# Linear attention into a SoLU layer on one core: w_out means on VectorE, tiles in any PSUM bank, and a new order

## The chip, the cores and the metric

The kernel runs on one core of a Trainium2 chip. The core has a matrix engine (TensorE, PE in the profile, with its weight loads as PEld), VectorE (DVE), ScalarE (ACT), GpSimd (POOL) and SyncE (SP), which work side by side, each through its own queue in program order, and wait for each other by semaphores. Matrix products land in PSUM, which has eight banks. The metric is the device time of one execution in microseconds (us), lower is better.

## The reference

Eight batches of eight heads with 576 tokens of 64 numbers; then one layer on the 4608 tokens of 512 numbers.

```python
kv = np.einsum('bhsd,bhse->bhde', k, v)
out = np.einsum('bhsd,bhde->bhse', q, kv)
rms = np.sqrt(np.mean(out * out, axis=-1, keepdims=True) + 1e-06)
x = (out / rms * g_norm)            # heads side by side: 4608 x 512
h = x @ w_in                        # 512 x 1024
e = np.exp(h - h_max)
solu = h * (e / (np.sum(e, axis=-1, keepdims=True) + 1e-09))
ln = (solu - mu) / np.sqrt(var + 1e-06) * g_ln
return ln @ w_out                   # 1024 x 512
```

## The kernel before, in words

The 4608 tokens are worked in nine chunks of 512, called c. Chunk c below 8 holds the first eight of every nine tokens of batch c; chunk 8 holds the ninth ones of all batches. A step's name carries its chunk: u.2.5 is the product u of chunk 2, piece 5.

For each batch, k, v and q are loaded by POOL's DMA queue with a cast to bf16 (`load`, L292; for batches 0 and 1 in two halves of four heads each). `kv_mm` (L333) multiplies k by v on 64 x 64 tiles; `kv_copy` (L346) brings the result to SBUF in two layouts, kvd[..., 0] and kvd[..., 1], in which the two heads of a pair lie in either half of the partitions. For batches 0 and 1 the matmuls give one layout only, and of three copies per half one is whole and two carry the crossed halves over. q is turned by PE (`qT_mm`, L368) for chunks 0 to 3 and by a transposing DMA on SP for the others. `o_mm` (L385) gives the attention output o, half hf and part z at a time. ACT squares it (sq), `s_mm` averages it over the head, ACT makes the reciprocal root (ln and ex; one instruction in chunk 0), and DVE multiplies (x, L422). So x of a chunk has four pieces, hf 0 and 1 by z 0 and 1.

The layer: `h_mm` (L459) multiplies the four row blocks of w_in by x for each of eight pieces f of 128 features; for chunks 0 to 2 each piece is cut in a first half (row blocks 0 and 1, which need only hf 0) and a second (2 and 3). ACT takes exp (L466), DVE multiplies h by it to u (L470), u is squared on POOL or ACT (usq, L474), and POOL adds pairs of exps (es, L478). `sums` (L498) adds u, usq and es over the features with 80 small matmuls; `turn`, `stats` and `rstd` make one scale per token from them. The softmax's divisor and the layer norm become that scale together with a mean taken out of w_out beforehand: w_out is loaded as fp32r (w_out_f), `w_mean` (L540) computes the mean over the features of g_ln times w_out with eight matmuls against g_mean, and `w_center` (L546) writes g_ln times w_out less that mean in bf16. `out_mm` (L557) multiplies u by it, four blocks m of 128 tokens a chunk; `scale` (ob, L564) multiplies by the token's scale, and `store` (L568) sends the block out, from SP's queue or, at the end, ACT's.

The last block, out.8.3, is computed in one bank; its scaling and store are cut in two halves of 256 columns (L590).

What sets the order of the work: every step is a named piece, and the string ORDER (L20) is one list by hand of all pieces; `emit` (L133) issues them in that order, so each engine's queue is the list cut down to its own pieces, POOL's and SP's DMA issues among them. A word such as usq.0.4:act picks the engine. PSUM is held by tags: h, out and o have two banks each, s and misc one each; HOME (L89) moves single tiles to another tag. A tile may take a bank when the earlier user of it is done. "warm" (L272) are matmuls on zeros with no use for the result: twelve at the start, then seven times two between the first steps. make_ident (L259) builds the identity on POOL behind seven loads; turn_g (L263) and all of PE behind it wait for that.

## Time and profile before

| | |
|---|---|
| median of 3 runs | 193.65 us (193.42 to 195.79) |
| span of the profiled execution, first to last instruction | 192.3 us |
| busy: PE, ACT, POOL, DVE | 93%, 76%, 67%, 58% |
| mean granted TensorE clock | 0.982 |
| moved by DMA | 29.71 MB, mean 154 GB/s |

Of the profiled execution the page gives the span; the runs' times also hold what lies before the first and after the last instruction. In the lines that follow, a group's line has line number, engine, operation, tiles written and read, shapes and count, then busy us and mean ns of one, then the idle time of the engine just before these instructions and who ended it. A matmul's mean holds its way through the array; a row of them follows each other faster: 12 of 128x512 take 2.59 us at full clock. A line of the windows has the stage, its length, busy us and count of PE, PEld, DVE, ACT and POOL, the granted clock, the share of the DMA engines and GB/s. A line of the timeline has start, duration, engine, line, operation and in brackets the idle time before it and its releaser.

### The profile page before, as it was taken

The numbers are of one execution on the slowest core, as the hardware profiler recorded it, in microseconds if no ns is written. First come the engines' busy times: TensorE is split into PE (matmuls) and PEld (weight loads), VectorE is DVE, ScalarE is ACT, GpSimd is POOL, SyncE is SP. The second block draws the span as 40 slices with busy tenths as digits, with TensorE's granted clock in tenths as the row PEclk, the third lists the DMA queues.
The fourth block names the chain that finished last, engine by engine and source line by source line (L and its number), as shares of the span: only waits on it lengthen the run. The fifth ranks groups of instructions, "written<-read, shape, count | busy, mean of one in ns | idle before, by whom it ended". The sixth has DMA issues, their size and how long they took to land.

```text
span 192.3 us, 5320 instructions
## 1 busy us (share of the span) xinstructions
PE 179.1 (93%) x2199; PEld 88.1 (46%) x2199; DVE 110.8 (58%) x228; ACT 146.3 (76%) x256; POOL 129.6 (67%) x138
## 2 busy tenths in 40 slices
PE   7697996999799999998999999999999999999991
...
PEclk9879998899999999999999999999999999999999
...
GB/s 51 187 205 206 206 336 290 208 207 209 206 185 186 241 162 200 201 271 176 170 209 251 33 16 197 201 81 111 75 15 55 29 139 0 109 112 0 162 61 218
DMA packets 35544, 29.71 MB, mean 154 GB/s; under 512 B 16440, under 2 KB 30016, under 8 KB 35520
## 3 DMA queue, kind: packets, MB, share of 16 engines
...
q10 hardware_dynamic: 144, 0.13, 0.2%
...
## 4 chain that ended last, share of the span: by engine, by line
PE 70%; DMA 9%; POOL 6%; ACT 5%; DVE 4%; issue 4%; POOLq 0%; ACTq 0%
PE h_ps L461 26%; PE out_ps L559 25%; DMA k_sb<-in_k_dram 9%; PE misc_ps L505 5%; PE o_ps L392 3%; PE s_ps L404 3%; ACT osq_sb L211 2%; PE misc_ps L340 2%; PE misc_ps L373 2%; POOL v_sb L295 2%; DVE x_sb L424 2%; PE out_ps L542 1%; PE s_ps L275 1%; POOL k_sb L295 1%; ACT e_sb L468 1%
## 5 line engine op out<-in xcount | busy, mean ns | idle before, releaser
L461 PE MATMUL h_ps<-x_sb,w_in_sb 128*128 128x512 bf16 x288 | 70.4, 381 | 0.1
L559 PE MATMUL out_ps<-w_out_sb,u_sb 128*128 128x512 bf16 x288 | 68.9, 379 | 0.1
L213 POOL TENSOR_TENSOR usq_sb<-u_sb 128x512 bf16<-128x512 bf16 x52 | 53.4, 1040 | 21.3 <-DVE u_sb L472 21.2
L472 DVE TENSOR_TENSOR u_sb<-h_ps,e_sb 128x512 bf16<-128x512 f32 x72 | 47.5, 685 | 23.0 <-ACT e_sb L468 19.9
L480 POOL TENSOR_TENSOR es_sb<-e_sb 128x512 bf16<-128x512 f32 x36 | 45.4, 1275 | 20.2 <-issue 11.9
L468 ACT ACTIVATE e_sb<-h_ps,zero_t 128x512 f32<-128x512 f32 x72 | 46.6, 687 | 11.7 <-PE h_ps L461 9.1
L559 PEld LDWEIGHTS <-u_sb 128*128 128x128 bf16 x288 | 27.4, 98 | 33.7 <-issue 2.1
L461 PEld LDWEIGHTS <-w_in_sb 128*128 128x128 bf16 x288 | 26.9, 98 | 32.2 <-issue 2.8
L424 DVE SCALAR_TENSOR_TENSOR x_sb<-o_ps,g_rep,rst_sb 128x512 bf16<-128x512 f32 x36 | 26.6, 747 | 19.8 <-ACT rst_sb L412 17.2
L211 ACT ACTIVATE osq_sb<-o_ps,zero_t 128x512 bf16<-128x512 f32 x36 | 23.3, 685 | 5.6 <-PE o_ps L392 5.6
L408 ACT ACTIVATE lss_sb<-s_ps,eps_t 128x512 f32<-128x512 f32 x32 | 21.2, 685 | 3.3 <-PE s_ps L404 3.1
L219 DVE TENSOR_SCALAR ob_sb<-out_ps,rstd 128x512 f32<-128x512 f32 (+1 forms) x21 | 15.3, 734 | 14.0 <-PE out_ps L559 11.0
L412 ACT ACTIVATE rst_sb<-lss_sb,zero_t 128x512 f32<-128x512 f32 x32 | 22.5, 720 | 0.4
L404 PE MATMUL s_ps<-osq_sb,head_mean 128*128 128x512 bf16 x36 | 13.5, 392 | 1.9 <-ACT osq_sb L211 1.9
L211 ACT ACTIVATE usq_sb<-u_sb,zero_t 128x512 bf16<-128x512 bf16 x20 | 13.8, 715 | 1.0 <-DVE u_sb L472 1.0
L505 PEld LDWEIGHTS <-stat_sel 128*32 128x32 bf16 x720 | 10.3, 97 | 5.4 <-issue 5.3
L217 ACT ACTIVATE ob_sb<-out_ps,rstd 128x512 f32<-128x512 f32 (+1 forms) x16 | 10.5, 672 | 2.5 <-PE out_ps L559 2.0
L207 ACT CAST kvd<-misc_ps 64x128 bf16<-64x128 f32 (+1 forms) x13 | 3.4, 260 | 10.9 <-PE misc_ps L340 8.2
L207 DVE CAST kvd<-misc_ps 64x128 bf16<-64x128 f32 (+1 forms) x17 | 4.9, 288 | 11.3 <-ACT kvd L207 11.0
L275 PE MATMUL s_ps<-zeros 128*128 128x512 bf16 x26 | 9.3, 495 | 1.2 <-DVE zeros L238 1.2
L392 PE MATMUL o_ps<-qT_sb,kvd 64*64 64x256 bf16 (+1 forms) x192 | 8.6, 253 | 1.7 <-DVE kvd L207 1.3
L340 PEld LDWEIGHTS <-k_sb 64*64 64x64 bf16 x576 | 7.1, 110 | 4.7 <-issue 3.8
...
## 6 DMA issues: line engine op xcount, KB each, us to landing
...
k_sb<-in_k_dram POOLq DMA_DIRECT2D x4, 288.0 KB, 10.5
...
```

Of the source, the lines that this page charges most:

```text
L211: nc.scalar.activation(out=dst, in_=src, func=AF.Square, bias=zero_t[:, :])
L213: on[engine].tensor_tensor(out=dst, in0=src, in1=src, op=MUL)
L404: nc.tensor.matmul(t[:, :], head_mean[:, :], T["osq", i][:, :], start=True, stop=True)
L408: nc.scalar.activation(out=t[:, :], in_=T["s", i][:, :], func=AF.Ln, bias=eps_t[:, :])
L412: nc.scalar.activation(out=t.rearrange("p a b c -> p (a b c)"), in_=T["lss", i][:, :], func=AF.Exp, scale=-0.5, bias=zero_t[:, :])
L424: nc.vector.scalar_tensor_tensor(out=t[:, 2 * hf:2 * hf + 2, z], in0=T["o", c, hf, z][:, :, :, :], scalar=g_rep[:, :], in1=T["rst", (c, hf ...
L461: nc.tensor.matmul(bank(("h", c, f), [128, 512])[:, :], w_in_sb[:, dt, f * 128:(f + 1) * 128], T["x", c][:, dt].rearrange("p a b c -> p (a ...
L468: nc.scalar.activation(out=t[:, f % 2, :], in_=T["h", c, f][:, :], func=AF.Exp, bias=zero_t[:, :])
L472: nc.vector.tensor_tensor(out=t[:, f, :], in0=T["h", c, f][:, :], in1=T["e", c, f // 2][:, f % 2, :], op=MUL)
L480: on[engine].tensor_tensor(out=t[:, n, :], in0=e[:, 0, :], in1=e[:, 1, :], op=ADD)
L505: nc.tensor.matmul(t[32 * j:32 * j + 32, 0, :], stat_sel[:, i, :], cols, start=(part == 0 and n == 0), stop=(part == 2 and n == n_src - 1) ...
L559: nc.tensor.matmul(bank(("out", c, m), [128, d_model])[:, :], T["u", c][:, f, m * 128:(m + 1) * 128], w_out_sb[:, f, :], start=(f == 0), s ...
```

## The change

- w_out is loaded as plain fp32. DVE adds up g_ln times w_out over four blocks at a time (w_add, eight instructions into w_acc and w_accr), and w_mean is one matmul for each half against a constant (mean_r). g_mean goes.
- The tags go: each of the eight banks is a tag of its own, and HOME names a bank for every PSUM tile.
- w_in is loaded in halves of its rows (row blocks 0 and 1, then 2 and 3) instead of its columns.
- For batches 0 and 1 kv_mm computes both layouts into two banks, twice the matmuls, and two whole copies replace the three.
- out.8.3 is computed as two halves of 256 columns in two banks, each with its own ob and store.
- usq may run on DVE. In the new order 35 of the 72 are on POOL, 12 on ACT and 25 on DVE; before it was 52 on POOL and 20 on ACT.
- The fill matmuls are given by FILL (name of the tile whose bank they use, count, columns). 26 of 512 columns stand first in PE's queue.
- ORDER is new throughout. The DMA queue of POOL begins v.0.0, (identity), q.0.0, k.0.0, q.0.1, v.0.1, k.0.1, w_in.0, w_in.1, q.1.0, k.1.0, v.1.0, w_out.1, v.1.1, q.1.1, k.1.1, w_out.0; before, all of batch 1 came ahead of w_out. store.8.1, store.8.2 and store.8.3.1 go by ACT's queue.
- pair_add and its names stand in the code, but PAIRED is empty and no such piece is made.

The diff, cut to its core; of ORDER the first and last lines of either side are shown.

```diff
 ORDER = """
-v.0.0 k.0.0 q.0.0 q.0.1 warm k.0.1 v.0.1 w_in.1 ident turn_g warm.0 kv_mm.0.0 warm.2 qT_mm.0.0 kv.0.0.0:act kv.0.0.1
-kv.0.0.2:act warm.3 qT.0.0 w_in.0 g_mean o_mm.0.0 warm.1 sq.0.0.1 q.1.0 warm.4 v.1.0 sq.0.0.0 s_mm.0.0.1 ex.0.0.1
-qT_mm.0.1 k.1.0 qT.0.1 warm.5 s_mm.0.0.0 kv_mm.0.1 ex.0.0.0 kv.0.1.1:act x.0.0.1 x.0.0.0 kv.0.1.0 kv.0.1.2 q.1.1 k.1.1
-warm.6 o_mm.0.1 sq.0.1.1 sq.0.1.0 v.1.1 s_mm.0.1.1 h.0.6.0 s_mm.0.1.0 h.0.4.0 ex.0.1.1 ex.0.1.0 x.0.1.1 x.0.1.0
-h.0.5.0 w_out.0 h.0.0.0 h.0.5.1 h.0.4.1 table w_out.1 exp.0.5 exp.0.4 h.0.6.1 h.0.1.0 es.0.2 h.0.0.1 exp.0.6 exp.0.0
-h.0.1.1 qT_mm.1.0 h.0.3.0 kv_mm.1.0 h.0.3.1 u.0.5 u.0.6 u.0.4 qT.1.0 u.0.0 exp.0.1 kv.1.0.0:act kv.1.0.2:act kv.1.0.1
-h.0.2.0 o_mm.1.0 qT_mm.1.1 h.0.2.1 h.0.7.0 u.0.1 exp.0.3 qT.1.1 u.0.3 sq.1.0.1 sq.1.0.0 exp.0.2 u.0.2 s_mm.1.0.0
-usq.0.6 h.0.7.1 ln.1.0.0 s_mm.1.0.1 kv_mm.1.1 exp.0.7 q.2.0 ln.1.0.1 kv.1.1.2:act kv.1.1.0 kv.1.1.1 ex.1.0.0 o_mm.1.1
-sq.1.1.1 usq.0.0 usq.0.2 k.2.0 es.0.0 x.1.0.0 ex.1.0.1 s_mm.1.1.1 sq.1.1.0 x.1.0.1 es.0.1 v.2.0 u.0.7 w_mean.0
-ln.1.1.1 s_mm.1.1.0 ex.1.1.1 h.1.5.0 w_mean.1 ln.1.1.0 x.1.1.1 h.1.0.0 w_center.5 ex.1.1.0 x.1.1.0 usq.0.1 h.1.2.0
-v.3.0 usq.0.4:act w_center.2 h.1.6.0 usq.0.7:act w_center.0 qT_mm.2.1 h.1.0.1 v.4.0 h.1.5.1 es.0.3 usq.0.3:act h.1.6.1
-h.1.1.0 h.1.2.1 exp.1.0 usq.0.5 k.3.0 k.4.0 exp.1.5 h.1.1.1 w_center.1 u.1.0 exp.1.6 exp.1.2 qT.2.1:act exp.1.1 u.1.5
...
-u.8.7 u.8.1 store.6.3 store.6.0 store.6.2 out.7.2.0 turn.7 store.6.1 exp.8.3 exp.8.2 out.7.1.0 h.8.5.1 out.7.1.1
-out.7.3.0 exp.8.5 stats.7 rstd.7 out.7.2.1 u.8.2 u.8.5 u.8.3 usq.8.5:act usq.8.2 out.7.3.1 usq.8.7:act out.7.0.0
-es.8.3 ob.7.1 ob.7.2 es.8.1 es.8.2 out.8.0.0 usq.8.1:act ob.7.3:act usq.8.3:act store.7.1 out.8.2.0 usq.8.4:act sums.8
-out.7.0.1 ob.7.0 turn.8 out.8.1.0 store.7.2 out.8.2.1 store.7.3 store.7.0 stats.8 out.8.0.1 out.8.3.0 out.8.1.1 rstd.8
-out.8.3.1 ob.8.2:act ob.8.0 ob.8.1:act store.8.0 store.8.2 store.8.1 ob.8.3.1:act ob.8.3.0 store.8.3.0:act store.8.3.1
+warm.2 warm.9 warm.4 warm.3 v.0.0 warm.0 ident turn_g q.0.0 qT_mm.0.0 qT.0.0 k.0.0 kv_mm.0.0 kv.0.0.1:act q.0.1
+qT_mm.0.1 v.0.1 kv.0.0.0:act qT.0.1 o_mm.0.0 sq.0.0.0 warm.1 g_ln s_mm.0.0.0 warm.6 sq.0.0.1 s_mm.0.0.1 ex.0.0.0
+x.0.0.0 ex.0.0.1 k.0.1 kv_mm.0.1 kv.0.1.0 w_in.0 w_in.1 kv.0.1.1:act o_mm.0.1 sq.0.1.1 warm.5 sq.0.1.0 s_mm.0.1.1
+ex.0.1.1 x.0.0.1 h.0.7.0 s_mm.0.1.0 h.0.0.0 q.1.0 h.0.5.0 ex.0.1.0 x.0.1.1 table h.0.2.0 h.0.3.0 x.0.1.0 h.0.2.1
+exp.0.2 u.0.2 h.0.0.1 exp.0.0 u.0.0 h.0.7.1 exp.0.7 h.0.1.0 h.0.1.1 u.0.7 h.0.5.1 h.0.3.1 exp.0.5 exp.0.1 exp.0.3
+qT_mm.1.0 k.1.0 v.1.0 kv_mm.1.0 kv.1.0.0:act h.0.6.0 w_out.1 qT.1.0 kv.1.0.1 v.1.1 u.0.3 q.1.1 h.0.4.0 u.0.5 o_mm.1.0
+h.0.4.1 k.1.1 u.0.1 w_add.4 sq.1.0.1 sq.1.0.0 h.0.6.1 s_mm.1.0.1 w_out.0 w_add.5 w_add.6 exp.0.6 u.0.6 es.0.3
+s_mm.1.0.0 ln.1.0.0 ex.1.0.0 x.1.0.0 warm.7 exp.0.4 u.0.4 usq.0.0 ln.1.0.1 ex.1.0.1 warm.8 qT_mm.1.1 kv_mm.1.1
+kv.1.1.1:act q.2.0 kv.1.1.0:act qT.1.1 o_mm.1.1 sq.1.1.1 sq.1.1.0 x.1.0.1 h.1.7.0 s_mm.1.1.1 ln.1.1.1 usq.0.1
+s_mm.1.1.0 es.0.0 w_add.7 ln.1.1.0 h.1.6.0 w_add.0 w_add.1 w_add.2 h.1.2.0 v.2.0 h.1.3.0 qT_mm.2.0 ex.1.1.1 k.2.0
+w_add.3 w_mean.0 w_mean.1 x.1.1.1 h.1.5.0 ex.1.1.0 es.0.1 q.3.0 x.1.1.0 qT.2.0:act h.1.3.1 exp.1.3 h.1.1.0 h.1.1.1
+exp.1.1 w_center.0 w_center.1 qT_mm.2.1 usq.0.7:dve usq.0.2 w_center.2 es.0.2 u.1.3 w_center.3 u.1.1 qT.2.1:act
+h.1.7.1 exp.1.7 h.1.5.1 usq.0.4 u.1.7 v.3.0 h.1.2.1 exp.1.2 exp.1.5 h.1.0.0 u.1.5 h.1.6.1 h.1.0.1 exp.1.0 u.1.0
+kv_mm.2.0 exp.1.6 kv.2.0.1:act u.1.2 kv.2.1.1:act h.1.4.0 h.1.4.1 exp.1.4 w_center.4 w_center.5 kv.2.0.2:act usq.0.6
+kv.2.1.0:act usq.0.5 w_center.7 usq.0.3 kv.2.1.2:act out.0.2.0 out.0.2.1 sums.0 kv.2.0.0:act o_mm.2.0 sq.2.0.0 k.3.0
+turn.0 sq.2.0.1 out.0.3.0 out.0.3.1 u.1.6 w_center.6 usq.1.6:dve v.4.0 out.0.3.2 k.4.0 u.1.4 s_mm.2.0.0 ln.2.0.0
+ex.2.0.0 out.0.2.2 out.0.2.3 s_mm.2.0.1 stats.0 rstd.0 out.0.3.3 out.0.0.0 x.2.0.0 usq.1.3 ln.2.0.1 ex.2.0.1 out.0.0.1
+out.0.0.2 ob.0.2 o_mm.2.1 kv_mm.3.0 out.0.0.3 sq.2.1.0 s_mm.2.1.0 usq.1.1:dve es.1.0 usq.1.7:dve x.2.0.1 usq.1.4
...
+turn.7 out.7.0.0 exp.8.2 u.8.2 exp.8.3 u.8.3 stats.7 usq.8.2:dve es.8.1 usq.8.3 out.7.1.0 out.7.1.1 store.6.3 rstd.7
+ob.7.1 store.7.1 h.8.7.1 exp.8.7 out.7.0.1 out.7.3.0 out.7.3.1 ob.7.3:act es.8.0 usq.8.5 out.8.1.0 ob.6.0:act ob.7.0
+out.7.2.0 out.7.2.1 usq.8.0:act ob.7.2:act store.7.0 store.6.0 u.8.4 store.7.3 es.8.3 store.7.2 u.8.7 usq.8.7:dve
+out.8.2.0 usq.8.4:dve usq.8.1:dve sums.8 turn.8 stats.8 rstd.8 out.8.1.1 ob.8.1:act store.8.1:act out.8.0.0 out.8.0.1
+ob.8.0:act store.8.0 out.8.2.1 ob.8.2 store.8.2:act out.8.3.0 ob.8.3.0:act store.8.3.0 out.8.3.1 ob.8.3.1:act
+store.8.3.1:act
 """
...
 HOME = """
-misc.g:s s.warm:misc misc.kv.0.0:h misc.kv.0.1:s misc.kv.1.1:s misc.kv.4.0:s s.kv.4.1:misc misc.kv.5.0:h misc.kv.6.0:h
...
+misc.g:4 misc.kv.0.0.0:6 misc.kv.0.0.1:7 misc.kv.0.1.0:4 misc.kv.0.1.1:5 misc.kv.1.0.0:0 misc.kv.1.0.1:2
...
+out.8.3.1:6 s.warm:4
 """
+FILL = {0: ("s.warm", 19, 512), 1: ("misc.kv.0.0.1", 18, 128), 2: ("o.0.0.1", 2, 512), 3: ("s.0.0.1", 1, 512), 4: ("s.0.0.0", 1, 512), 5: ("misc.kv.0.1.1", 9, 128), 6: ("o.0.1.1", 2, 512), 7: ("misc.kv.1.1.1", 24, 128), 8: ("o.1.1.1", 3, 512), 9: ("s.1.1.1", 3, 512)}
+PAIRED = ()
...
-            self.homes[by_word[word]] = tag
+            self.homes[by_word[word]] = "b" + tag
...
-    banks = {"h": 2, "out": 2, "o": 2, "s": 1, "misc": 1}
+    banks = {f"b{i}": 1 for i in range(8)}
...
-    w_out_f = big.tile([128, NF, d_model], FP32R, name="w_out_f")
+    w_out_f = big.tile([128, NF, d_model], FP32, name="w_out_f")
+    w_acc = big.tile([128, 2, d_model], FP32, name="w_acc")
+    w_accr = big.tile([128, 2, d_model], FP32R, name="w_accr")
+    mean_r = big.tile([128, 128], FP32R, name="mean_r")
...
-    g_mean = big.tile([128, NF, 128], FP32R, name="g_mean")
+    nc.vector.memset(mean_r.bitcast(FP32), 1.0 / d_ff)
...
-    def make_g_mean(_):
+    def take_g(_):
         nc.vector.tensor_copy(g_ln_sb[:, :], T["misc", "g"][:, :])
-        nc.vector.tensor_scalar_mul(
-            out=g_mean[:, :, :], in0=g_ln_sb[:, :, None].to_broadcast([128, NF, 128]), scalar1=1.0 / d_ff
-        )
...
-        cols = slice(half * d_ff // 2, (half + 1) * d_ff // 2)
-        nc.gpsimd.dma_start(w_in_sb[:, :, cols], moe_w_in[:, cols].rearrange("(n p) f -> p n f", p=128))
+        ns = slice(half * NP // 2, (half + 1) * NP // 2)
+        nc.gpsimd.dma_start(w_in_sb[:, ns, :], moe_w_in.rearrange("(n p) f -> p n f", p=128)[:, ns])
...
-                        rows, y = slice(64 * r, 64 * r + 64), r ^ (x if b > 1 else 0)
-                        nc.tensor.matmul(
-                            bank(kv_key(b, x), [128, 2, D])[64 * y:64 * y + 64, m, :],
-                            T["k", b][rows, n, i, :], T["v", b][rows, n, i, :],
-                            start=(m == 0 and i == 0), stop=(i == 8), skip_group_check=True,
-                        )
+                        rows = slice(64 * r, 64 * r + 64)
+                        for w in range(2) if b < 2 else (0,):
+                            y = r ^ (w if b < 2 else x)
+                            nc.tensor.matmul(
+                                bank(kv_key(b, x, w), [128, 2, D])[64 * y:64 * y + 64, m, :],
+                                T["k", b][rows, n, i, :], T["v", b][rows, n, i, :],
+                                start=(m == 0 and i == 0), stop=(i == 8), skip_group_check=True,
+                            )
...
     def kv_copy(engine, b, x, part):
-        y = x if b > 1 else 0
+        if b < 2:
+            copy(engine, kvd[:, b, part, kv_pairs(b, x), :], T[kv_key(b, x, part)][:, :, :])
+            return
         src = T[kv_key(b, x)]
...
-                add(("h", c, f, 0), "pe", lambda _, c=c, f=f: h_mm(c, f, (0, 1)), [("w_in", f // 4), *xs[0]], [("x", c), ("h", c, f)])
-                add(("h", c, f, 1), "pe", lambda _, c=c, f=f: h_mm(c, f, (2, 3)), [("h", c, f, 0), *xs[1]], [("x", c), ("h", c, f)])
+                add(("h", c, f, 0), "pe", lambda _, c=c, f=f: h_mm(c, f, (0, 1)), [("w_in", 0), *xs[0]], [("x", c), ("h", c, f)])
+                add(("h", c, f, 1), "pe", lambda _, c=c, f=f: h_mm(c, f, (2, 3)), [("h", c, f, 0), ("w_in", 1), *xs[1]], [("x", c), ("h", c, f)])
...
-            add(("usq", c, f), "pool|act", lambda e, c=c, f=f: u_sq(e, c, f), [("u", c, f)], [("u", c), ("usq", c)])
+            add(("usq", c, f), "pool|act|dve", lambda e, c=c, f=f: u_sq(e, c, f), [("u", c, f)], [("u", c), ("usq", c)])
...
+    def w_add(n):
+        half, i = divmod(n, NF // 2)
+        by = dict(in0=w_out_f[:, n, :], scalar=g_ln_sb[:, n:n + 1], in1=w_acc[:, half, :], op0=MUL, op1=ADD)
...
+        if i == 0:
+            nc.vector.tensor_scalar_mul(out=w_acc[:, half, :], in0=w_out_f[:, n, :], scalar1=g_ln_sb[:, n:n + 1])
+        else:
+            nc.vector.scalar_tensor_tensor(out=(w_accr if i == NF // 2 - 1 else w_acc)[:, half, :], **by)
...
     def w_mean(half):
-        for f in range(half * NF // 2, (half + 1) * NF // 2):
-            nc.tensor.matmul(
-                bank(("out", "mean"), [128, d_model])[:, :], g_mean[:, f, :], w_out_f[:, f, :], start=(f == 0), stop=(f == NF - 1)
-            )
+        nc.tensor.matmul(
+            bank(("out", "mean"), [128, d_model])[:, :], mean_r[:, :], w_accr[:, half, :], start=(half == 0), stop=(half == 1)
+        )
...
+    for n in range(NF):
+        half, i = divmod(n, NF // 2)
+        add(("w_add", n), "dve", lambda _, n=n: w_add(n), [("w_out", half), "g_ln"] + ([("w_add", n - 1)] if i else []))
+    for half in range(2):
+        add(("w_mean", half), "pe", lambda _, half=half: w_mean(half),
+            [("w_add", half * NF // 2 + NF // 2 - 1)] + [("w_mean", 0)] * half, [("out", "mean")])
...
+            if (c, m) == (LAST, 3):
+                for x in range(2):
+                    cols, half = slice(x * d_model // 2, (x + 1) * d_model // 2), (*key, x)
+                    add(("out", c, m, x), "pe", lambda _, half=half, cols=cols: out_mm(half, range(NF), cols),
+                        [("w_center", f) for f in range(NF)] + [("u", c, f) for f in range(NF)], [("u", c), half])
+                    add(("ob", c, m, x), "dve|act", lambda e, half=half, cols=cols: scale(e, half, cols),
+                        [("out", c, m, x), ("rstd", c)], [half, ("ob", c, m)])
+                    add(("store", c, m, x), "sp|act", lambda e, c=c, m=m, cols=cols: store(e, c, m, cols), [("ob", c, m, x)], [("ob", c, m)])
+                continue
...
+    def warm(key, n, cols):
+        kind = key[1] if key[0] == "misc" else key[0]
+        if kind == "qT":
+            t = bank(key, [128, 2, 4, 128], BF16)
+            for i in range(n):
+                nc.tensor.transpose(t[:, 0, i % 4, :], zeros[:, 0:128], ident[:, :])
+            return
+        t = bank(key, {"kv": [128, 2, D], "o": [128, 2, 4, 64]}.get(kind, [128, 512]))
+        flat = t.rearrange("p a b -> p (a b)") if kind == "kv" else t.rearrange("p a b c -> p (a b c)") if kind == "o" else t
+        for _ in range(n):
+            nc.tensor.matmul(flat[:, 0:cols], zeros[:, 0:128], zeros[:, 0:cols], start=True, stop=True)
```

## The prediction

> **What bounds the kernel now.** I read the page's busy time and its 40 slices first, then windows by stage, then the timeline of the first 60 us and of the last 10, then groups by line for durations.
>
> ```profile
> span 192.3 us, 5320 instructions
> PE 179.1 (93%) x2199; PEld 88.1 (46%) x2199; DVE 110.8 (58%) x228; ACT 146.3 (76%) x256; POOL 129.6 (67%) x138
> PE   7697996999799999998999999999999999999991
> PEclk9879998899999999999999999999999999999999
> ```
> TensorE is the bound from about 36 us on; only the start, a few short waits and the end can give time back. The windows (first columns: stage, its length, PE busy; then the granted clock) place them:
>
> ```profile
> 5.00:10.00 5.00, 3.28 (x45) 1.65 (x43) 0.29 (x1) 0.34 (x2) 4.79 (x11) 0.82 1.19 190
> 30.00:35.00 5.00, 3.69 (x16) 1.98 (x17) 3.17 (x6) 4.24 (x8) 4.97 (x6) 0.71 1.26 243
> 40.00:50.00 10.00, 8.40 (x192) 4.70 (x190) 8.04 (x14) 7.70 (x15) 8.47 (x9) 1.00 1.21 208
> 90.00:100.00 10.00, 9.22 (x197) 4.91 (x198) 6.01 (x16) 8.34 (x17) 8.72 (x10) 1.00 1.35 181
> 150.00:160.00 10.00, 10.00 (x152) 5.00 (x151) 7.04 (x15) 7.80 (x13) 7.75 (x8) 1.00 0.34 81
> 185.00:192.30 7.30, 3.48 (x17) 1.37 (x14) 1.24 (x2) 2.42 (x5) 0.00 (x0) 1.00 0.54 181
> ```
> Between 35 and 185 us PE idles about 3 us in all: 1.6 in 40 to 50, 1.2 in 80 to 110. In the timeline the waits have names:
>
> ```profile
> 7.42 0.22 PE L264 MATMUL misc_ps<-eye,g_rows 8*128 8x8 f32 x1 [1.72 <-POOL eye masks.py:199]
> 32.03 2.26 PE L542 MATMUL out_ps<-w_out_f,g_mean 128*128 128x512 f32 x4
> 49.53 0.24 PE L505 MATMUL misc_ps<-usq_sb,stat_sel 128*32 128x128 bf16 x4 [1.57 <-issue]
> 188.52 0.47 ACT L217 ACTIVATE ob_sb<-out_ps,rstd 128x256 f32<-128x256 f32 x1 [0.17 <-PE out_ps L559]
> 189.02 0.48 DVE L219 TENSOR_SCALAR ob_sb<-out_ps,rstd 128x256 f32<-128x256 f32 x1 [2.29 <-ACT ob_sb L217]
> ```
> PE stands until POOL has built the identity; it runs the w_out means at the low clock of 30 to 35; sums.0 waits for late squares; and at the end VectorE starts its half of the last bank only when ScalarE has left it. Prices of the moved work:
>
> ```profile
> L213 POOL TENSOR_TENSOR usq_sb<-u_sb 128x512 bf16<-128x512 bf16 x52 | 53.4, 1040 | 21.3 <-DVE u_sb L472 21.2
> L472 DVE TENSOR_TENSOR u_sb<-h_ps,e_sb 128x512 bf16<-128x512 f32 x72 | 47.5, 685 | 23.0 <-ACT e_sb L468 19.9 <-PE out_ps L559 2.9
> L547 DVE SCALAR_TENSOR_TENSOR w_out_sb<-w_out_f,g_ln_sb,out_ps 128x512 bf16<-128x512 f32 x8 | 5.6, 742 | 1.3 <-PE out_ps L542 1.3
> L207 DVE COPY qT_sb<-misc_ps 128x1024 bf16<-128x1024 bf16 x6 | 4.1, 686 | 2.9 <-PE misc_ps L373 2.9
> ```
>
> **The change, part by part.**
>
> *Loads and the first chain.* Loads that cast to bf16 move 206 GB/s (windows of 1 us), and 2.75 MB lie ahead of the end of w_in in both kernels, so w_in is whole at 19.4 us as now (PE's weight load at 19.41 waits for it). Halving w_in by rows costs nothing: five first halves need only w_in.0. POOL builds the identity before its second load: 0.9 us of POOL (6.44 to 7.36 now). The first load's 0.295 MB keep the DMAs busy 1.4 us meanwhile, so I take 0.2 late, between 0 and 0.9. In exchange the 1.72 us wait goes. PE opens with 26 fill matmuls. Now eight cost 0.43 each from 1.2 us and later ones 0.22, so 26 end near 8.5, about when q.0.0 lands (qT_mm.0.0's data came by 9.6 as third load; now it is second). o_mm.0.0 comes at 11.4 instead of 11.87, o_mm.0.1 at 15.0 instead of 16.3, and the last x of chunk 0 by 18.8. The second halves of h.0 start at 19.5 instead of 20.44.
>
> *kv in both layouts (b below 2).* 144 more matmuls, but a kv_mm of 72 on four tiles took 0.70 us (43.88 to 44.58) and one of 36 on two tiles 0.64 to 0.85, so PE pays about 0, at most 4 x 0.7. Twelve copies become eight; those left are 0.27 to 0.3 each, about 0.3 us off each of four chains, already in the times above.
>
> *Chunk 1.* From 19.4: q, k, v of its first half (0.85 MB) land at 23.5, w_out.1 at 26.1 (1.05 MB at the 400 GB/s of 26 to 30 us), the second half at 30.2, w_out.0 at 32.8, q.2 at 35.4. kv_mm.1.1 so runs at 30.2 where it ran at 28.7: this is the price of w_out.1 ahead of it. Then kv copies to 31.5, o_mm to 31.9, on ACT two squares, two ln, two exp at 0.64 to 0.72 to 36.1. On DVE w_add.0 to 3 wait for w_out.0 at 32.8, with x.1.1.1 and x.1.1.0 queued behind them, and all second halves of h.1 behind those. A w_add is the row of 742 ns with its PSUM input in SBUF; the first of each half is one-input, 0.42 from g_mean's 694 ns for 1024 columns (bounds 0.35 and 0.75): 0.42 + 3 x 0.74 = 2.6, done at 35.5. So x.1.1.0 ends at 36.9. PE meanwhile does five first halves of h.1, qT_mm.2.0 (waits q.2 to 35.4, w_mean and h.1.5.0 behind it) and the two w_mean. Of the w_mean, six matmuls go: 1.4 us at 0.23, but in a stretch where PE waits for chunk 1 anyway. POOL's q.2.0 stands behind es.0.3, which waits for exp.0.6 at 27.4; issued by 30.5 it still moves right behind w_out.0.
> Now: 36.53, one first half of h.1 done. After: 36.9, with four halves (4 x 0.43) and one qT_mm (0.45) more. Net **-1.8 us**, bounds -3.5 (clock and DMA a little better) and +1.5 (w_adds at 1 us and a late q.2).
>
> *36 to 59 us.* sums.0 moves behind two pieces of out.0, when its squares are through POOL (43) and bank 1 is free (u.1.2, 44.6): the 1.57 us wait goes. New waits: h.1.0.0 for bank 3 (u.1.3, 0.5), out.0.0.0 for bank 0, kv_mm.3.0 for bank 4 (ob.0.2), 0.2 to 0.4 each, all behind DVE's queue of w_center, u and x. Net **-0.4**, bounds -1.5 and +2.
>
> *Squares.* 52 on POOL become 35, 20 on ACT become 12, 25 are on DVE. POOL falls by 17 x 1.04 to 112 us, ACT by 8 x 0.715 and two ob to about 139. A DVE square is unshown: 0.34 (half the 1024-column bf16 copy) to 0.69 (u). I take 0.5, between equally near rows: 12.5, with w_add 5.3, ob 1.5, less copies and g_mean 2.1: DVE about 128 (67%). No engine passes PE, so I set the stretch from 59 to 188 at **0**: in it 1.4 us of waits stand (0.78 at 90, a wait for k). Any bank for any tile could remove those and some of the handover cost; a new order can make others. Bounds -3 and +6.
>
> The Trainium skill's page "SBUF — State Buffer" (section "SBUF: two separate sides") speaks against this part: it says that a VectorE instruction with two SBUF inputs and a GpSimd instruction reading SBUF take one port pair in turn, the loser fully waiting. No run here shows it; every tensor pair that DVE reads now has a PSUM member. By it the sum would be that of rival 2; without it, the sum here.
>
> *The last tokens.* out.8.3 goes to two banks: 16 matmuls of 256 columns instead of 8 of 512, the same columns, 0 (at most 0.2 for eight more loads). ob.8.3.0 runs under the second half, and the second ob no longer stands behind the first: the 0.5 us from 188.52 to 189.02 goes. The final issue stays on ACT, 2.8 us from ob to the end as now; store.8.1 and store.8.2 move to that queue ahead of it, 0.4 to 0.6 each, the last about 0.4 us before PE ends. Net **-0.5**, bounds -0.7 and +0.5.
>
> Sum: 192.3 - 1.8 - 0.4 + 0 - 0.5 = 189.6 us of span. The runs' median of 193.65 lies 1.35 above the span shown; so 191.0.
>
> **Rivals.**
> 1. *The free banks also clear the middle.* Speaks for it: ACT and POOL get lighter, and two or three banks per kind is what ties h, out and o now. Against: only 1.4 us of idle are visible from 59 us on. Taking that and as much again in handovers: 191.0 - 3 = 188.0.
> 2. *DVE's squares and adds collide with POOL (ends slower).* 33 new DVE instructions read two SBUF tensors. If each has to wait out a POOL one: POOL would be busy 58% of the time, in instructions of 1.04 to 1.275 us, so 33 x 0.58 x 0.55 = 10.5 us of standing on DVE. Place: w_add.0 to 3 (x.1.1 behind), usq.1.x before x.2.x, and the squares of chunks 3 to 8. For: at 35.5, 48.5 and 58 DVE is last in my own working. Against: DVE would be at 139 us, 73%, less than ACT now at 76%, which PE outlives with 3 us of idle. With half to two thirds reaching PE it is 196 to 198. It eats the gain at 2.7 us (0.08 per instruction) and is slower by 2% from 6.6 us (0.2 each).
> 3. *The clock falls twice.* PE does about 2.6 us of work between 31.9 and 36.9 in my schedule; before, work of 0.49, 0.48 and 0.23 in 29 to 32 was followed by 3.4 us at half clock. That again, 1.7 us, and a start in which fill stays slow some 2 us longer (26 x 0.43 would end at 12.4) gives 193.5. The Trainium skill ("TensorE: Matmul & The Clock Gate", Part 1) calls the window free-running, which would make this vary between runs; the eight slow matmuls in 3.4 us agree with its length.
>
> **Numbers.** Forecast 0.38 (189.3 to 193), rival 1 0.25 (186 to 189.5), rival 2 0.26 (193.5 to 200), rival 3 0.11. The range 186.5 to 197.0 leaves out a tenth of rival 1 and half of rival 2, 0.16 in all; the forecast's own range is 189.3 to 193. A measurement of this kernel tells about 2% from no change: faster is below 189.8, slower above 197.5. Rival 1 whole and a sixth of the forecast make faster 0.31; under half of rival 2 makes slower 0.12; the rest, 0.57, is within.
>
> **What would show it.** Right: no wait of PE for the identity; h.0 second halves at 19.5; the first full second half of h.1 at 36 to 38 with five first halves done; no wait before sums.0; DVE squares at 0.34 to 0.69; 0.5 us less from the last matmul to the end. Wrong: PE waiting for x or u behind a w_add or a DVE square longer than 0.7 us (rival 2); a granted clock under 0.9 after 8 us (rival 3); PE idle under 1 us from 59 on (rival 1). The forecast falls if landing times shift, most of all k.1.1's and w_out.0's.

## The result: 7% slower, and the profile after

The changed kernel takes 207.7 us (207.3 to 209.4, 4 runs) where the kernel before took 194.7 beside it: a ratio of 1.071, 95% interval 1.063 to 1.079. The forecast was 191.0, its range ended at 197.0. The profiled execution has a span of 206.0 us and a time of 207.8. Here and below, the times in us are medians of all runs, while a ratio leaves out the executions in which the chip was in a slower state.

The page of after, its busy line and two of its slices:

```profile
span 206.0 us, 5701 instructions
PE 179.1 (87%) x2377; PEld 90.7 (44%) x2401; DVE 143.6 (70%) x258; ACT 140.7 (68%) x247; POOL 115.6 (56%) x121
PE   7987896329995998899999799989999999989990
PEclk9999999955999999999999999999999999999998
```

TensorE has the same 179.1 us of busy time as before, in a span that is 13.7 us longer: what came is idle time, most of it in the eighth and ninth slice (36 to 46 us) and the thirteenth, where PE reads 3, 2 and 5; the clock is at half in the ninth and tenth. VectorE is busy 143.6 us where the prediction had 128. The windows of after (stage, its length, then PE, PEld, DVE, ACT, POOL busy, then the granted clock; POOL's time here holds its DMA issues as well as its computing):

```profile
30.00:35.00 5.00, 3.23 (x99) 2.10 (x98) 5.00 (x7) 3.67 (x8) 4.98 (x6) 1.00 0.59 147
35.00:40.00 5.00, 2.50 (x16) 1.03 (x14) 4.96 (x3) 3.75 (x6) 4.97 (x6) 1.00 1.18 188
40.00:50.00 10.00, 4.92 (x15) 2.21 (x16) 9.81 (x11) 0.85 (x2) 9.51 (x10) 0.51 1.17 188
60.00:70.00 10.00, 7.59 (x122) 4.01 (x120) 9.54 (x14) 7.42 (x16) 9.97 (x11) 1.00 0.80 116
80.00:90.00 10.00, 8.16 (x151) 3.96 (x151) 7.34 (x16) 7.41 (x15) 9.95 (x11) 1.00 0.96 143
```

From 35 to 40 us VectorE is "busy" 4.96 of 5 us with only three instructions, whose lines elsewhere take 0.5 to 0.75 us each. In the last three stages POOL is busy almost throughout and PE is not. The timeline of after shows it (start, length, engine, line, what ended the wait ahead of it):

```profile
27.98 0.47 DVE L571 TENSOR_SCALAR w_acc<-w_out_f,g_ln_sb 128x512 f32<-128x512 f32 x1
28.49 0.75 DVE L573 SCALAR_TENSOR_TENSOR w_acc<-w_out_f,g_ln_sb,w_acc 128x512 f32<-128x512 f32 x1
...
33.41 0.73 DVE L439 SCALAR_TENSOR_TENSOR x_sb<-o_ps,g_rep,rst_sb 128x512 bf16<-128x512 f32 x1
33.71 1.27 POOL L500 TENSOR_TENSOR es_sb<-e_sb 128x512 bf16<-128x512 f32 x1
34.07 2.11 DVE L573 SCALAR_TENSOR_TENSOR w_accr<-w_out_f,g_ln_sb,w_acc 128x512 fp32r<-128x512 f32 x1
36.11 2.59 DVE L571 TENSOR_SCALAR w_acc<-w_out_f,g_ln_sb 128x512 f32<-128x512 f32 x1
36.47 1.29 POOL L500 TENSOR_TENSOR es_sb<-e_sb 128x512 bf16<-128x512 f32 x1
38.74 4.84 DVE L573 SCALAR_TENSOR_TENSOR w_acc<-w_out_f,g_ln_sb,w_acc 128x512 f32<-128x512 f32 x2
43.62 1.41 DVE L573 SCALAR_TENSOR_TENSOR w_accr<-w_out_f,g_ln_sb,w_acc 128x512 fp32r<-128x512 f32 x1
45.08 1.22 PE L576 MATMUL out_ps<-w_accr,mean_r 128*128 128x512 f32 x2 [6.97 <-DVE w_accr L573]
47.66 0.41 DVE L230 TENSOR_TENSOR usq_sb<-u_sb 128x512 bf16<-128x512 bf16 x1
```

The first two w_adds of the kernel, at 28 us, when POOL computes nothing, take 0.47 and 0.75 us, near the forecast's prices. The third begins at 29.28, just behind POOL's first es (29.21), and takes 1.75. The other five, from 34 us on, with POOL computing and issuing loads by turns, take 2.11, 2.59, 1.40, 3.40 and 1.41; the 4.84 at 38.74 are two of them. The x at 33.41, whose o lies in PSUM, has POOL's es beside it too and takes its usual 0.73. POOL's own instruction at 36.47 is hardly longer (1.29 against 1.27): here it is VectorE that stands. POOL loses less, but not nothing: of its 30 computations beside w_adds and VectorE's squares, 11 are 0.2 to 0.45 us longer. So w_add.0 to 3 end at 45.0, where the forecast's price of 2.6 us from the same start at 36.1 would have given 38.7, and w_mean, first in TensorE's queue, waits 6.97 us. After that wait the clock is at half until 50.5 (granted 0.50 up to 50, 0.76 from 50 to 51).

The groups of after by line, with the mean in ns behind the bar; the last line is another view, in which the shortest, the median and the longest of the four stand behind the count:

```profile
L573 DVE SCALAR_TENSOR_TENSOR w_acc<-w_out_f,g_ln_sb,w_acc 128x512 f32<-128x512 f32 x4 | 7.3, 1828 | 0.1
L573 DVE SCALAR_TENSOR_TENSOR w_accr<-w_out_f,g_ln_sb,w_acc 128x512 fp32r<-128x512 f32 x2 | 3.5, 1761 | 0.0
L571 DVE TENSOR_SCALAR w_acc<-w_out_f,g_ln_sb 128x512 f32<-128x512 f32 x2 | 3.1, 1534 | 0.0
L230 DVE TENSOR_TENSOR usq_sb<-u_sb 128x512 bf16<-128x512 bf16 x25 | 21.8, 882 | 0.2
L573 DVE SCALAR_TENSOR_TENSOR w_acc<-w_out_f,g_ln_sb,w_acc x4: 751/1579/3404, 28.5 to 40.2; 128x512 f32<-128x512 f32 x4
```

The eight w_adds cost 13.9 us instead of 2 x 0.47 + 6 x 0.75 = 5.4; the 25 squares 21.8 instead of 25 x 0.41 = 10.3. Of the 25 squares, the eleven beside which POOL computes nothing take 0.41 to 0.57 us, and the fourteen beside a POOL computation take 0.73 to 1.73. Two of the fourteen have a load's issue beside them too; each of the other twelve ends 0.28 to 0.29 us behind the end of POOL's computation, whenever it began itself, as this one:

```profile
101.95 1.26 POOL L500 TENSOR_TENSOR es_sb<-e_sb 128x512 bf16<-128x512 f32 x1
102.44 1.05 DVE L230 TENSOR_TENSOR usq_sb<-u_sb 128x512 bf16<-128x512 bf16 x1
```

So a square waits for the whole of what POOL has under way, and what it is longer by is what was left of that.

### The profile page after: what moved, and what is told of

It is laid out like the page before. It is cut to its first block, busy times and chain, and to the rows that moved or that the text cites. A ratio compares the mean times of both kernels' runs of the same rounds, so it can differ in the third digit from the quotient of the medians.

```text
span 206.0 us, 5701 instructions
## 1 busy us (share of the span) xinstructions
PE 179.1 (87%) x2377; PEld 90.7 (44%) x2401; DVE 143.6 (70%) x258; ACT 140.7 (68%) x247; POOL 115.6 (56%) x121
## 4 chain that ended last, share of the span: by engine, by line
PE 32%; DMA 22%; DVE 22%; ACT 10%; issue 6%; POOL 5%; ACTq 0%; SPq 0%; POOLq 0%; DVEq 0%
PE out_ps L598 16%; DMA k_sb<-in_k_dram 11%; PE h_ps L476 10%; DMA v_sb<-in_v_dram 7%; DVE u_sb L487 7%; ACT e_sb L483 3%; DMA qT_sb<-q_sb 3%; DVE w_acc L573 3%; DVE usq_sb L230 3%; DVE x_sb L439 2%; POOL es_sb L500 2%; ACT lss_sb L423 2%; ACT rst_sb L427 2%; DVE ob_sb L236 2%; DVE w_accr L573 2%
## 5 line engine op out<-in xcount | busy, mean ns | idle before, releaser
L598 PE MATMUL out_ps<-w_out_sb,u_sb 128*128 128x512 bf16 (+1 forms) x286 | 66.7, 373 | 4.2 <-DVE x_sb L439 2.2
L230 POOL TENSOR_TENSOR usq_sb<-u_sb 128x512 bf16<-128x512 bf16 x35 | 37.8, 1092 | 22.6 <-DVE u_sb L487 22.6
L439 DVE SCALAR_TENSOR_TENSOR x_sb<-o_ps,g_rep,rst_sb 128x512 bf16<-128x512 f32 x36 | 26.6, 746 | 15.0 <-ACT rst_sb L427 10.5
L236 DVE TENSOR_SCALAR ob_sb<-out_ps,rstd 128x512 f32<-128x512 f32 x23 | 17.0, 746 | 7.6 <-PE out_ps L598 6.7
L230 DVE TENSOR_TENSOR usq_sb<-u_sb 128x512 bf16<-128x512 bf16 x25 | 21.8, 882 | 0.2
L224 ACT CAST kvd<-misc_ps 128x128 bf16<-128x128 f32 (+1 forms) x23 | 5.7, 261 | 13.9 <-PE misc_ps L350 11.5
L234 ACT ACTIVATE ob_sb<-out_ps,rstd 128x512 f32<-128x512 f32 (+1 forms) x14 | 9.0, 653 | 4.6 <-PE out_ps L598 2.4
L531 PEld LDWEIGHTS <-stat_sel 128*32 128x32 bf16 x720 | 10.2, 97 | 3.8 <-issue 3.8
L224 DVE COPY qT_sb<-misc_ps 128x1024 bf16<-128x1024 bf16 x6 | 4.0, 687 | 10.3 <-PE misc_ps L388 10.3
L228 ACT ACTIVATE usq_sb<-u_sb,zero_t 128x512 bf16<-128x512 bf16 x12 | 8.6, 719 | 2.2 <-DVE u_sb L487 2.2
L407 PE MATMUL o_ps<-qT_sb,kvd 64*64 64x256 bf16 (+1 forms) x192 | 7.2, 250 | 2.9 <-DMA qT_sb<-q_sb 1.1
L350 PE MATMUL misc_ps<-v_sb,k_sb 64*64 64x64 bf16 x720 | 8.0, 194 | 1.9 <-DMA k_sb<-in_k_dram 1.2
```

What stands on the lines that cost most here:

```text
L228: nc.scalar.activation(out=dst, in_=src, func=AF.Square, bias=zero_t[:, :])
L230: on[engine].tensor_tensor(out=dst, in0=src, in1=src, op=MUL)
L236: nc.vector.tensor_scalar_mul(out=dst, in0=src, scalar1=by)
L439: nc.vector.scalar_tensor_tensor(out=t[:, 2 * hf:2 * hf + 2, z], in0=T["o", c, hf, z][:, :, :, :], scalar=g_rep[:, :], in1=T["rst", (c, hf ...
L598: nc.tensor.matmul(bank(key, [128, d_model])[:, cols], T["u", c][:, f, m * 128:(m + 1) * 128], w_out_sb[:, f, cols], start=(f == 0), stop= ...
```

## The experiments

Each expectation sets theories against each other by the time that they give. Theory T: VectorE's instructions whose operands all lie in SBUF wait for POOL's, and through w_mean and x reach TensorE. Rivals: the new order itself is late in places (O), or the other edits cost (E). The runs were made on several chips, with the kernel before beside each; its medians there lie from 194.7 to 196.6, so ratios are compared.

**The sum of w_add in PSUM.** The running sum goes to a PSUM bank, so that no w_add reads two SBUF tensors or writes SBUF from one alone; w_add.7 moves behind x.1.0.1, and the fill of FILL 9 takes another bank.

```diff
-        by = dict(..., in1=w_acc[:, half, :], op0=MUL, op1=ADD)
+        acc = bank(("misc", "wacc", half), [128, d_model])
+        by = dict(..., in1=acc[:, :], op0=MUL, op1=ADD)
```

> The changed kernel with one difference: the running sums of w_add live in PSUM, not in SBUF, so each w_add reads one SBUF tensor instead of two. Count, order and DVE's work stay. Theory T (a VectorE instruction with two SBUF inputs and a POOL instruction take turns): w_add.0 to 3 fall from 8.9 us together to about 2.6 to 3.2, PE's wait of 7.0 us before w_mean shrinks to 1 to 2, time 199 to 201 against 207.7. Theory O (the new order and bank map cost the time, the adds only stand where nothing covers them): under 1.5 us of gain, 206 to 208.

Measured: 201.0 us, ratio 1.031 (1.020 to 1.042). From the timeline of acc_psum, w_add.7 (at 32.80) and the same four adds:

```profile
32.74 1.27 POOL L499 TENSOR_TENSOR es_sb<-e_sb 128x512 bf16<-128x512 f32 x1
32.80 0.74 DVE L573 SCALAR_TENSOR_TENSOR w_accr<-w_out_f,g_ln_sb,misc_ps 128x512 fp32r<-128x512 f32 x1
33.74 0.75 DVE L571 TENSOR_SCALAR misc_ps<-w_out_f,g_ln_sb 128x512 f32<-128x512 f32 x1 [0.20 <-DMA w_out_f<-in_moe_w_out_dram]
34.53 1.55 DVE L573 SCALAR_TENSOR_TENSOR misc_ps<-w_out_f,g_ln_sb,misc_ps 128x512 f32<-128x512 f32 x2
35.50 1.29 POOL L499 TENSOR_TENSOR es_sb<-e_sb 128x512 bf16<-128x512 f32 x1
36.12 0.75 DVE L573 SCALAR_TENSOR_TENSOR w_accr<-w_out_f,g_ln_sb,misc_ps 128x512 fp32r<-128x512 f32 x1
```

The one at 32.80 lies wholly beside POOL's es, the last two for the most part, and each takes 0.74 to 0.78 us; TensorE's wait for them is gone. T holds for w_add: some 3.9 of the 7.1%. What then ends last ahead of w_mean is the load of q.2, for which TensorE waits 2.88 us:

```profile
38.82 0.62 PE L387 MATMUL misc_ps<-ident,q_sb 128*128 128x128 bf16 x8 [2.88 <-DMA q_sb<-in_q_dram]
```

What follows is about the other 3.2%.

**Means on TensorE again.** w_add is taken out and the means are computed by 8 matmuls with g_mean, as before; all else is the new kernel.

```diff
-        nc.tensor.matmul(bank(("out", "mean"), ...), mean_r[:, :], w_accr[:, half, :], ...)
+        for f in range(half * NF // 2, (half + 1) * NF // 2):
+            nc.tensor.matmul(bank(("out", "mean"), ...), g_mean[:, f, :], w_out_f[:, f, :], ...)
```

> The changed kernel with w_add taken out: the means come from eight matmuls against g_mean on PE as in the kernel before; squares stay on VectorE. Theory T: like the sums in PSUM or 1 us better or worse, 198 to 201: eight matmuls cost PE 1.4 us more where it waits anyway, DVE loses 5 to 14 us. Theory O: 205 to 208.

Measured: 200.1 us, 1.032 (1.023 to 1.042): w_add in PSUM costs no more than no w_add, and what is left is not w_add.

**VectorE's 25 squares on ScalarE**, in the new kernel (sq_on_act) and with the sum in PSUM (both).

```diff
-usq.0.7:dve  (and 24 others)
+usq.0.7:act
```

> The changed kernel with its 25 squares of VectorE on ScalarE, at the same places of the order; w_add as it is. ScalarE gets 25 x 0.72 = 18 us more. Theory T: the stalls of PE at 60 to 70, 80 to 90, 130 to 140 and 180 to 190 (about 6 us) go for the most part, the long wait before w_mean stays: 202 to 204. Theory O: they stay or grow behind the longer ScalarE queue: 207 to 212.

> Both edits at once: sums of w_add in PSUM, squares on ScalarE; everything else of the change stays (banks, order, kv in both layouts, w_in by rows, last tokens in two banks, loads). Theory T: 192 to 196, the blind sum of 191 plus a ScalarE that is 18 us fuller. Theory O: 204 or more. If T is only half the story: 197 to 203.

Measured: 208.7 us, 1.075 (1.065 to 1.084), and 200.6, 1.029 (1.018 to 1.040). T, which asked for 202 to 204 and 192 to 196, fell for the squares: against after and acc_psum the ratio moved by +0.4 and -0.2 of a per cent, inside the intervals. In sq_on_act ScalarE was busy 154.9 us instead of 140.7.

**The squares on POOL, left out, and loads earlier**, all three with the sum in PSUM.

```diff
-usq.0.7:dve  (and 24 others)
+usq.0.7:pool            # sq_on_pool
+                        # no_dve_sq: gone, the sums read u
-es.0.3 usq.0.0 q.2.0 ... v.2.0 k.2.0
+q.2.0 v.2.0 k.2.0 es.0.3 usq.0.0   # loads_ahead, on sq_on_pool
```

> The kernel after with the sums of w_add kept in a PSUM bank (as in acc_psum, 201.0 us) and the 25 squares of VectorE moved to POOL, so that VectorE has no operation left that reads two operands from SBUF. Theory S (what is still lost beyond the 7 us of w_add, some 6 us, is the collision of VectorE's squares with POOL): 195 to 198 us, VectorE's busy time down by more than the 21.8 us that the squares took. Theory O (the rest lies in the new order: late loads, late joins of stages, the end): 200 to 204 us, as POOL now has 60 squares and the es sums behind them.

> As sq_on_pool, but the 25 squares that VectorE computed are left out altogether; the sums read u in their place, so the output is not the reference's. No engine does them, so this bounds from below what any placing of these squares can give in this order. Theory S: 194 to 197 us. Theory O: 199 to 202 us, no more than 2 us under acc_psum's 201.0.

> As sq_on_pool, and the loads q.2.0, v.2.0 and k.2.0 are issued on POOL's queue ahead of es.0.3 and usq.0.0, which they stood behind. Theory L (part of the rest is the wait of 2.3 to 3.7 us of qT_mm.2.0 for q.2): 1.5 to 3 us below sq_on_pool. Against it (the wait is hidden by a later one, for x of chunk 1): within 0.7 us of sq_on_pool.

Measured: 213.2 us, 1.075 (1.060 to 1.090); 198.7, 1.010 (1.004 to 1.015); 209.7, 1.067 (1.055 to 1.078). On POOL the squares are worst, beyond both theories. Left out they give 2.2% back, between what S and O asked for: so their work, and not only its collisions, finds no free place in this order on any of the three engines tried. Even without them the kernel is not faster than before. The earlier loads gained 0.9%, inside the intervals.

**The same test in the order of before**: its 20 squares of ScalarE on VectorE.

```diff
-usq.0.4:act  (and 19 others)
+usq.0.4:dve
```

> The kernel before, nothing changed but that its 20 squares of ScalarE are computed on VectorE. If VectorE's squares beside POOL's are what costs (theory S): 196 to 200 us, squares of 0.9 us on VectorE. If they do no harm in an order where VectorE has room (theory O): 193 to 196 us.

Measured: 197.2 us, 1.006 (1.001 to 1.010). From its page:

```profile
L213 DVE TENSOR_TENSOR usq_sb<-u_sb 128x512 bf16<-128x512 bf16 x20 | 13.9, 708 | 0.0
```

They are lengthened here too (0.71 against 0.41 alone), and cost about 1 us (0.6%), which is theory O. TensorE does wait for VectorE's u and ob in the profiled execution, 4.6 us in all against 0.2 in before; why no more of it shows in the time was not tried. This run also has the other turn, a square that begins first:

```profile
173.02 0.42 DVE L213 TENSOR_TENSOR usq_sb<-u_sb 128x512 bf16<-128x512 bf16 x1
173.09 1.49 POOL L480 TENSOR_TENSOR es_sb<-e_sb 128x512 bf16<-128x512 f32 x1 [6.23 <-issue]
```

The square that began 0.07 us ahead of POOL's es keeps its 0.42 us, and here the es is longer, 1.49 instead of 1.27.

**All edits in the old order.** The order, the engines and, but for the new tiles, the banks of the kernel before; w_add.0 to 3 right ahead of w_mean.0 and 4 to 7 ahead of w_mean.1, with the sum in SBUF, in PSUM, or left out for TensorE's 8 matmuls. So these three differ in the means alone.

```diff
-u.0.7 w_mean.0
+u.0.7 w_add.0 w_add.1 w_add.2 w_add.3 w_mean.0
-h.1.5.0 w_mean.1
+h.1.5.0 w_add.4 w_add.5 w_add.6 w_add.7 w_mean.1
```

> All edits of the change but the order: row halves of w_in, early kv in both layouts (the doubled kv tiles in banks free at that time), last tokens in two banks, w_add on VectorE reading its sum from SBUF, four of them right ahead of each w_mean; everything else in the order, on the engines and in the banks of the kernel before. Theory A (what costs is w_add's two SBUF operands beside POOL, wherever it stands): 5 to 9 us over the kernel before, a ratio of 1.025 to 1.045, with w_adds of 1.5 to 3.4 us. Theory B (in the old order POOL is idle or PE has other work there): a ratio of 0.99 to 1.01.

> As old_order_sbuf, with the running sum of w_add in a PSUM bank. Theory O (of the 3% that acc_psum still lost, most is the new order): a ratio of 0.985 to 1.01 to the kernel before. Theory E (the edits themselves lose it): 1.02 to 1.035, as acc_psum (1.031).

> As old_order_sbuf, with the means computed by 8 matmuls on TensorE as before and w_add left away: row halves, both layouts of kv and two banks for the last tokens in the old order. Theory O: a ratio of 0.98 to 1.0, the forecast's start (up to 1.8 us) and last tokens (0.5 us) found here. Theory E: 1.02 or more, as pe_means (1.032) in the new order.

Measured: 204.8 us, 1.049 (1.038 to 1.060); 201.8, 1.030 (1.016 to 1.044); 194.7, 0.999 (0.994 to 1.003). The first is theory A's outcome, a little above its range (1.045), and the last puts E out: row halves, both layouts and two banks cost nothing. The same edits with the means on TensorE are 0.999 in the old order and 1.032 in the new one: the new order, with its banks, engines and fill, costs 3.3%. In the timeline of old_order_sbuf POOL turns from computing to issuing DMAs while VectorE adds:

```profile
36.15 2.55 DVE L570 SCALAR_TENSOR_TENSOR w_acc<-w_out_f,g_ln_sb,w_acc 128x512 f32<-128x512 f32 x1
36.86 1.28 POOL L497 TENSOR_TENSOR es_sb<-e_sb 128x512 bf16<-128x512 f32 x1
38.74 1.41 DVE L570 SCALAR_TENSOR_TENSOR w_accr<-w_out_f,g_ln_sb,w_acc 128x512 fp32r<-128x512 f32 x1
39.55 1.55 POOL L300 DMA_DIRECT2D k_sb<-in_k_dram  x2
40.30 0.76 PE L573 MATMUL out_ps<-w_accr,mean_r 128*128 128x512 f32 x1 [8.33 <-DVE w_accr L570]
40.62 1.54 DVE L570 SCALAR_TENSOR_TENSOR w_acc<-w_out_f,g_ln_sb,w_acc 128x512 f32<-128x512 f32 x2
```

As soon as POOL only issues loads, two adds take 1.54 us together, as they would alone (0.75 each); the issues lie over the first of them. The 1.030 of old_order_psum lies in E's range, but not for E's reason, as the same edits without the adds give 0.999: that adds of the usual length would cost 3% was expected by neither theory. In its timeline and windows:

```profile
36.91 0.77 PE L573 MATMUL out_ps<-w_accr,mean_r 128*128 128x512 f32 x1 [4.74 <-DVE w_accr L570]
```

```profile
36.00:37.00 1.00, 0.10 (x1) 0.13 (x1) 0.99 (x2) 0.00 (x0) 0.99 (x2) 0.50 1.18 189
40.00:45.00 5.00, 5.00 (x18) 2.37 (x19) 3.83 (x6) 1.44 (x3) 0.77 (x2) 0.50 1.20 200
45.00:46.00 1.00, 1.00 (x4) 0.40 (x3) 0.25 (x1) 0.81 (x2) 0.00 (x0) 0.64 1.20 204
```

Four adds of 0.75 us right ahead of w_mean.0 are 3 us on TensorE's path, in a stretch where it had little else to do: it waits 4.74 us, and the clock is at half until 45.7, 8.8 us after work resumed (with a pause of 0.87 us in it, for w_mean.1). At half clock 8 us of matmuls hold 4 us of work. So 3 us of VectorE in that place, twice, cost 3.1%, some 6 us.

**Squares behind x, and loads earlier, with the means on TensorE.** Both are edits of the order of pe_means: nine squares change place with the x behind them, and the loads of chunk 2 go ahead of es.0.3; both_moved has the two.

```diff
-usq.1.1:dve es.1.0 usq.1.7:dve x.2.0.1
+es.1.0 x.2.0.1 usq.1.1:dve usq.1.7:dve
```

The reason for them stood in the timeline of pe_means:

```profile
52.74 3.19 DVE L229 TENSOR_TENSOR usq_sb<-u_sb 128x512 bf16<-128x512 bf16 x2
54.37 3.92 POOL L499 TENSOR_TENSOR es_sb<-e_sb 128x512 bf16<-128x512 f32 x3
55.86 0.74 DVE L438 SCALAR_TENSOR_TENSOR x_sb<-o_ps,g_rep,rst_sb 128x512 bf16<-128x512 f32 x1
56.66 1.47 PE L586 MATMUL out_ps<-w_out_sb,u_sb 128*128 128x512 bf16 x6 [2.09 <-DVE x_sb L438]
```

Two squares take 3.19 us instead of 0.82, x stands behind them, and TensorE behind x, for 2.09 us.

> The kernel of pe_means (the new order, the means by 8 matmuls on TensorE; ratio to the kernel before 1.032), with 9 of VectorE's 25 squares moved behind the x that they stand ahead of on VectorE, among them the two (usq.1.1, usq.1.7) that take 3.19 us ahead of x.2.0.1. Theory S (those squares, lengthened beside POOL, hold x back and TensorE with it): TensorE's wait of 2.1 us for x in front of out.0.1 gone, a ratio of 1.015 to 1.025. Theory V (VectorE is simply full from 40 to 60 us, a square later only moves the wait): 1.027 to 1.037.

> The kernel of pe_means with q.2.0, v.2.0 and k.2.0 issued on POOL's queue ahead of es.0.3 and usq.0.0. Theory L (late loads hold chunk 2 back): 1 to 2.5 us less, a ratio of 1.018 to 1.027, as loads_ahead gained 0.9% on sq_on_pool. Against it: 1.028 to 1.036.

> Both moves, sq_behind_x and loads_early, on pe_means. If S and L both hold: 1.0 to 1.015. If neither: 1.027 to 1.037. If the order is late in many small places that these two do not touch, 1.018 to 1.027.

Measured: 201.5 us, 1.035 (1.024 to 1.046); 200.7, 1.027 (1.009 to 1.044); 199.8, 1.022 (1.005 to 1.039). Theory S fell for this place, and the timeline of sq_behind_x says why:

```profile
55.39 2.07 DVE L229 TENSOR_TENSOR usq_sb<-u_sb 128x512 bf16<-128x512 bf16 x1
57.38 0.74 DVE L235 TENSOR_SCALAR ob_sb<-out_ps,rstd 128x512 f32<-128x512 f32 x1
58.17 0.77 PE L349 MATMUL misc_ps<-v_sb,k_sb 64*64 64x64 bf16 x72 [1.81 <-DVE ob_sb L235]
```

One square later by an instruction, lengthened to 2.07, now holds ob back, whose bank kv_mm waits for. The 2.09 us became 1.81. Whether the loads are worth 0.5 or 1% the intervals do not tell.

**What the edits are worth.** In old_order_pe the largest late wait of TensorE is new: 2.23 us for k.6, 0.55 before. Three loads go ahead of usq.2.5 on POOL (old_order_k_early), and sums.0 behind out.0.3.0 as well (old_order_two); before_two has both moves in the kernel before.

```diff
-v.6.0 ... usq.2.5 ... v.5.0 k.5.0 es.2.3 k.6.0
+v.6.0 ... v.5.0 k.5.0 k.6.0 usq.2.5 ... es.2.3
-sums.0 ... out.0.3.0
+... out.0.3.0 sums.0
```

> The kernel of old_order_pe (row halves, both layouts and two banks in the old order, means on TensorE; ratio 0.999) with the loads v.5.0, k.5.0 and k.6.0 issued on POOL ahead of usq.2.5 instead of behind it and es.2.3. If TensorE's wait of 2.23 us for k.6 is not covered by something else that is late: 1.5 to 2.3 us less, a ratio of 0.986 to 0.992. If another wait takes its place: 0.995 to 1.003.

> As old_order_k_early, and sums.0 moved behind out.0.3.0 on TensorE, so that its wait of 1.92 us for the squares and es of chunk 0 lies beside those 0.9 us of matmuls. 0.5 to 1.0 us under old_order_k_early if POOL ends them by then; nothing if stats.0 then comes too late for the first ob.

> The kernel before with the same two moves and none of the change's edits. Its waits there were 0.55 us for k and 1.57 us in front of sums.0, so 0.8 to 1.5 us less, a ratio of 0.992 to 0.996. If old_order_two is lower than this by over 0.5 us, the edits of the change are worth something; if not, they are worth nothing.

Measured: 194.7 us, 0.993 (0.986 to 0.9995); 194.7, 0.996 (0.991 to 1.001); 195.5, 1.004 (0.999 to 1.008). The moves bring nothing in the kernel before, and sums.0's place nothing at all. old_order_two lies 0.8% under before_two, their intervals all but apart: with the moves the three edits may hold about 1.5 us, though by themselves (old_order_pe) they show none. old_order_k_early is the fastest version of this study, by 0.7% under before, hardly more than the measurement tells.

## Why the prediction was wrong, step by step

*Two steps failed: the price of w_add, and the 0 set for the new order from 59 to 188 us.* The first is "0.42 + 3 x 0.74 = 2.6, done at 35.5": w_add.0 to 3 took 8.9 us (36.11 to 45.03), and x.1.1.0, forecast for 36.9, ended at 46.3. The row of 742 ns that it came from reads one of its tensors from PSUM. The prediction itself said that no run showed an instruction of VectorE with two SBUF tensors, and then took the price of the nearest row, with 1 us as the most that an add could take. acc_psum and old_order_psum, with 0.75 each, show that it was the place of the operand. That place is worth 3.8% in the new order (1.071 / 1.031); in the old one it is 1.8% (1.049 / 1.030), with intervals that overlap.

*The squares and the zero from 59 to 188 us.* 0.5 us each was taken, 0.88 measured, and 143.6 us of VectorE instead of 128. "No engine passes PE" was true and decided nothing: no engine's share is near TensorE's, and yet in pe_means VectorE is busy 19.5 of the 20 us from 40 to 60. TensorE's waits of 0.3 us and more after 50 us sum to 8.1 us in six places of pe_means, and to 0.55 in the kernel before. The loss of the order (pe_means: 3.2%, 6 us) is as large as the stage's upper bound of +6, where the sum had 0. VectorE is only half of it: by what ended them, 3.8 of the 8.1 us are waits for its x and u, 3.7 for transposed loads of q, 0.7 for ScalarE. The waits of TensorE in pe_means, and in no_dve_sq, both from 50 us on (what it waited for: sum, times, longest):

```profile
PE o_ps L406 <- DMA qT_sb<-q_sb: 3.7, 2, 2.0
PE out_ps L586 <- DVE x_sb L438: 2.1, 1, 2.1
PE o_ps L404 <- DMA qT_sb<-q_sb: 2.7, 2, 1.7
```

In no_dve_sq (the last line) the waits for x and u are gone, and 3.7 us of waits for loads (2.7 for transposed q, 1.0 for k) are the most of what is left. The prediction wrote that "a new order can make others", and its sum put them at nothing.

*Rival 2 was the right mechanism, under-priced.* It gave 10.5 us of standing on VectorE (for 33 instructions with two SBUF tensors; by the prediction's own count of one-input adds they are 31); the adds stood 13.9 - 5.4 = 8.5 and the squares 21.8 - 10.3 = 11.5, so 20. Its POOL share of 58% is a mean of the whole span: six of the eight adds run after 29 us, and from 30 to 50 POOL is busy 19.5 of 20 us, 6.2 of them with DMA issues. And its "half to two thirds" reaching PE left out the clock. The Trainium skill ("SBUF — State Buffer", section "SBUF: two separate sides") describes such an exclusive lock for VectorE with two SBUF inputs, and for its two-port modes with one. The rows of after agree: 0.75 against 1.40 to 3.40 us for two inputs, 0.47 against 2.59 for one, and 0.73 unchanged for the x from PSUM.

*Rival 3 came as a consequence.* In after the clock fell while TensorE waited 7 us for w_add, and from 45.08 to 50.5 work ran at half, 2.7 us of it lost. Without that wait it differs by execution: in the profile of pe_means the granted clock of every 10 us stage up to 190 us is 1.00, while in acc_psum it is at half for 3.4 us from 40.1, behind the wait for q.2, which costs the 1.7 us that rival 3 named.

*The start.* PE's wait for the identity went, as said. But the slow fill lasted to 6.2 us, 12 matmuls, not 8 (in pe_means, with the same start, to 4.0 us and 7 matmuls, and o_mm.0.0 was hardly earlier, 12.01, so the fill was not what held it); o_mm.0.0 came at 12.47 instead of 11.4; w_in was whole at 20.87 instead of 19.4, and the second halves of h.0 began at 20.9 instead of 19.5. The step "0.2 late" for the loads was too small; why they are 1.5 late I did not try. q.2.0, to be issued "by 30.5", left POOL at 31.9 behind es.0.3 and usq.0.0. Chunk 1's x.1.1.0 ends at 38.2 even in acc_psum, where 36.9 was forecast.

*36 to 59 us.* The wait ahead of sums.0 is gone, as forecast. One of the new ones, "0.2 to 0.4 each", is 2.2 us: out.0.1 for the bank that x.2.0.1 clears, behind two lengthened squares.

*The last tokens.* The second ob no longer waits, as forecast. From the last matmul to the end it was 4.9 us in after, 3.5 in pe_means, against 3.9 before: a gain of the size forecast is inside that spread, so this is not settled.

*Open.* What in the new order loses its 3.3% is shown in part: 2.2 points go when VectorE's squares are left out. Moving squares, or the loads of chunk 2, does not bring the rest back; the waits lie in six places, and taking one away showed the next. The traces point to one more place, which no run tested. In ten of the eleven profiles with the new order TensorE waits 1.0 us or more for a transposed q (twice in pe_means, for chunks 4 and 6), in none of the eight with the old order. POOL issues q.6 at 97.1 us in pe_means, at 66.9 in before:

```profile
97.12 0.81 POOL L302 DMA_DIRECT2D q_sb<-in_q_dram  x1
110.81 0.63 PE L406 MATMUL o_ps<-qT_sb,kvd 64*64 64x256 bf16 x16 [1.98 <-DMA qT_sb<-q_sb]
```

Issuing q.4 and q.6 earlier is the move that I would try next. I did not try the order with the old engine of each square and copy either.
